# Late modulation vectors as packed rows, reciprocal broadcasts on ScalarE's queue, and a last tile in three pieces

## The chip, the cores and the metric

The kernel runs on one core of a Trainium2 chip. The metric is device time in microseconds of one execution; lower is better. The times shown for a version are medians of repeated runs, and a version's profile comes from one further execution.

## The reference

A transformer block with modulation vectors that depend on a condition c. All large tensors are bfloat16.

```python
mod = silu(c) @ w_mod                     # (1,1024) @ (1024, 6*1024): sa, ca, ga, sb, cb, gb
h = layernorm(x) * (1 + ca) + sa          # x: 2048 x 1024
q = h @ wq                                # 32 heads of 128
p = softmax(q k^T / sqrt(128))            # 4 kv heads, the last 512 keys of the cache
x = x + ga * ((p v) @ wo)                 # wo: 4096 x 1024
h = layernorm(x) * (1 + cb) + sb
x = x + gb * ((silu(h @ w_gate) * (h @ w_up)) @ w_down)   # inner width 3584
```

Six vectors of 1024 values come out of w_mod. sa and ca are needed at once, for the first layernorm. ga is needed when the attention output of the first rows is complete, sb and cb for the second layernorm, and gb only at the very end of the block: these four are the *late* vectors.

## The kernel before

The 2048 rows are worked in four chunks (cc = 0 to 3) of 512 rows, and a chunk in four tiles of 128 rows. Each chunk has 32 attention heads, so the attention part is a loop over 128 steps k, one head of one chunk each (NU = 128, H = 32).

In a step, `emit_s(k)` computes the scores of head k for 512 keys (4 matmuls into two s_ps buffers) and ScalarE turns them into pT by exp. VectorE adds pT up over the keys in two instructions (psA, then psB). `emit_q(k + 3)` computes the queries three heads ahead (8 matmuls of 512 columns, q_ps), and VectorE copies them out of PSUM (qT). `emit_o(k - 1)` multiplies pT by the values (4 matmuls, o_ps), and ScalarE copies o_ps to oT. Every fourth step, `emit_l` sums psB over the partitions for four heads at once: four matmuls with 32 output columns each, every one in its own quarter of the TensorE array and of one PSUM bank (l_ps). ScalarE then takes Ln and Exp of it (the reciprocal, rinv) and stores four rows of it to DRAM (r_d). `load_rb` reads these rows back, repeated over all 128 partitions (rb, two loads of 512 KB), and `emit_norm` on VectorE multiplies oT by rb. From step 12 on, `emit_wo` adds one part of the output projection per step (8 matmuls, a_ps), which VectorE collects in acc.

Other work is hung on the steps through a table of tasks: `at(k, f, ...)` puts a call of f after the queries of step k. In this way are placed: the loads of w_mod (`load_wm`), the late vectors' products (`mod_cols`, `mod_bcast`), the layernorm of the next chunk (`plan_ln`: bn_stats, xn, a DMA transpose into hT, then eight scale-and-shift instructions on VectorE), the loads of x, and an estimate of the scores' bound (`bound_wq`: 32 sums of squares of wq tiles on VectorE, all in chunk 0; `bound_k`: 16 sums of squares of k_ld tiles, at step 10), which decides at the end whether another path of the kernel has to be run.

A column product (`mod_cols`) has 32 matmuls with w_mod as the stationary operand and one moving column. It gives 512 values of a vector as columns (128 partitions x 4), as layernorm's scale and shift are used. A broadcast product (`mod_bcast`) has silu(c), repeated over 128 columns, as the stationary operand (silrep) and w_mod as the moving one; it takes 8 matmuls of 512 columns and gives 512 values on all 128 partitions, as ga and gb are used (ga_bc, gb_bc).

After the attention loop come, chunk by chunk, the gated projections (`emit_gu`: gu_ps, sg, guT) and the down projection (`emit_down`: 28 matmuls into d_ps, then on VectorE f = d_ps * gb and o_sb = f + x, then a store of 128 x 512 values from ScalarE's queue).

The order in which each engine takes its instructions is not that of the code alone. A scheduler places them by priority (the order of the code) and by its own estimate of when they are ready; on the chip each engine then runs its list strictly in order. Tiles come from pools with a fixed number of buffers. The ones that matter here: PSUM tag "mm" with 4 banks, shared by q_ps, o_ps, a_ps, l_ps, d_ps and the modulation products; "hT" with 4 buffers of 1 MB, shared by the w_mod tiles and the hT of the chunks; "rb" with 2; blkB (7 buffers; kT and v_sb hold two of them, and five are left for wq tiles); blkC (10: oT, wo).

Nearly all loads are issued on SyncE's queue, which waits in order for the buffers it fills; in the kernel before, only the load of c and the stores of r_d and of the output are issued by ScalarE.

Of the kernel before, what the change touches and what calls it, by code (L numbers as in the profile page):

```python
# [9 lines left out]
ALU = mybir.AluOpType  # L10
AX = mybir.AxisListType
BF16 = mybir.dt.bfloat16
FP32 = mybir.dt.float32
# [575 lines left out]
def fast_path(ctx, tc, flag, A_x, A_k_cache, A_v_cache, A_wq, A_wo, B_x, B_w_gate, B_w_up,  # L589
# [3 lines left out]
    nc = tc.nc  # L593
    P = 128
    _, S, D = A_x.shape
    _, Hkv, Sk, Dh = A_k_cache.shape
    HD = A_wq.shape[1]
    H = HD // Dh
# [4 lines left out]
    TCW = 512  # L603
    NTC = S // TCW
    QT = TCW // P
    DT = D // P
    FT = F // P
    WT = W // P
    DH = D // 512
# [7 lines left out]
    x2d = A_x.flatten_outer_dims()  # L617
    out2d = out.flatten_outer_dims()
# [5 lines left out]
    wm_v = w_mod.rearrange("(dt p) n -> p dt n", p=P)  # L624
# [4 lines left out]
    const = ctx.enter_context(tc.tile_pool(name="const", bufs=1))  # L629
    xpool = ctx.enter_context(tc.tile_pool(name="xres", bufs=1))  # L630
    hpool = ctx.enter_context(tc.tile_pool(name="hT", bufs=4))
# [3 lines left out]
    wk = ctx.enter_context(tc.tile_pool(name="work", bufs=2))  # L635
    sm = ctx.enter_context(tc.tile_pool(name="small", bufs=4))
    psp = ctx.enter_context(tc.tile_pool(name="psum", bufs=4, space=bass.MemoryType.PSUM))
    dp = ctx.enter_context(tc.tile_pool(name="dram", bufs=4, space=bass.MemoryType.DRAM))
# [7 lines left out]
    def blkC(name, shape, dt=BF16):  # L646
        return pc_.tile(shape, dt, name=name, tag="C")

    def mm(name, shape=(P, 512), dt=FP32):
        return psp.tile(list(shape), dt, name=name, tag="mm", bufs=4)  # L650
# [4 lines left out]
    def load(out, in_, eng=None):  # L655
        with nc.allow_non_contiguous_dma(reason="weight slice"):
            (eng or nc.sync).dma_start(out=out, in_=in_)
# [5 lines left out]
    nc.scalar.dma_start(out=c_r, in_=c_v)  # L663
    xt = [xpool.tile([P, D], BF16, name=f"x{tt}", tag=f"x{tt}") for tt in range(S // P)]

    def load_x(cc):
        for t in range(cc * QT, (cc + 1) * QT):
            nc.sync.dma_start(out=xt[t], in_=x2d[t * P:(t + 1) * P, :])

    wm_tiles = {}  # L670

# [7 lines left out]
    def load_wq(cc, hg, parts=(0, 1)):  # L679
        for i in parts:  # L680
            t = blkB("wq", [P, 4, 512])
            load(t, wq_v[:, 4 * i:4 * i + 4, hg * 512:(hg + 1) * 512])
            wq_tiles[(cc, hg, i)] = t

    load_x(0)
    for half in range(DH):
        load_wm(1, half)
        load_wm(0, half)
# [5 lines left out]
    for kv in range(Hkv):  # L694
        load(v_sb[:, kv], v_v[:, kv])
    load_wq(0, 1)
    load_x(1)


    ident = const.tile([P, P], BF16, name="ident")  # L700
# [1 line left out]
    ones_bf = const.tile([P, P], BF16, name="ones_bf")  # L702
# [4 lines left out]
    sa, ca1, sb, cb1 = (modT[:, i, :] for i in range(4))  # L707
    ga_bc = const.tile([P, D], FP32, name="ga_bc")
    gb_bc = const.tile([P, D], FP32, name="gb_bc")


    ec = sm.tile([DT, P], FP32, name="ec", tag="ec", bufs=2)
    nc.scalar.activation(out=ec, in_=c_r, func=ACT.Exp, scale=-1.0)
    nc.vector.tensor_scalar(out=ec, in0=ec, scalar1=1.0, scalar2=None, op0=ALU.add)
    rc = sm.tile([DT, P], FP32, name="rc", tag="ec", bufs=2)
    nc.vector.reciprocal(out=rc, in_=ec)
    sil_r = const.tile([DT, P], BF16, name="sil_r")
    nc.vector.tensor_tensor(out=sil_r, in0=c_r, in1=rc, op=ALU.mult)
# [2 lines left out]
    siluc = const.tile([P, DT], BF16, name="siluc")  # L721
# [9 lines left out]
        nc.vector.tensor_scalar(out=dst[:, 4 * half:4 * half + 4], in0=ps,  # L731
                                scalar1=1.0 if add_one else 0.0, scalar2=None, op0=ALU.add)

    rep_t = {}

    def mod_bcast(vec, half, dst):
        if "r" not in rep_t:
            r = wk.tile([P, DT, P], BF16, name="silrep", tag="xn", bufs=3)
            for dt in range(DT):
                nc.vector.tensor_scalar(out=r[:, dt, :], in0=ones_bf,  # L740
                                        scalar1=siluc[:, dt:dt + 1], scalar2=None, op0=ALU.mult)
            rep_t["r"] = r
        wm = wm_tiles.pop((vec, half))
        ps = mm("bc_ps")
        for dt in range(DT):
            nc.tensor.matmul(ps, lhsT=rep_t["r"][:, dt, :], rhs=wm[:, dt, :],
                             start=(dt == 0), stop=(dt == DT - 1))
        nc.vector.tensor_copy(out=dst[:, half * 512:(half + 1) * 512], in_=ps)

    tasks = {}  # L750

    def at(k, f, *a):
        tasks.setdefault(k, []).append((f, a))


    hT = {}
# [12 lines left out]
    def ln_norm(tt, on_act=False):  # L769
        mv = ln.pop(tt)  # L770
        n = wk.tile([P, D], BF16, name="xn", tag="xn", bufs=3)
        if on_act:
            nc.vector.scalar_tensor_tensor(out=mv[:, 3:4], in0=mv[:, 0:1], scalar=-1.0,
                                           in1=mv[:, 2:3], op0=ALU.mult, op1=ALU.mult)
            nc.scalar.activation(out=n, in_=xt[tt], func=ACT.Identity, bias=mv[:, 3:4],
                                 scale=mv[:, 2:3])
        else:
            nc.vector.tensor_scalar(out=n, in0=xt[tt], scalar1=mv[:, 0:1], scalar2=mv[:, 2:3],
                                    op0=ALU.subtract, op1=ALU.mult)
        return n  # L780

    xn = {}
# [24 lines left out]
    def plan_ln(k, key, sc, sh):  # L807


        for t in range(QT):  # L810
            tt = key[1] * QT + t
            at(k + 2 * t, ln_stats, tt)
            at(k + 2 * t + 1, ln_rows, tt)
            at(k + 2 * t + 2, ln_xpose, key, tt)
        for dt in range(DT):
            at(k + 11 + dt, ln_mod, key, dt, sc, sh)
# [14 lines left out]
    for t in range(QT):  # L831
        ln_stats(t)
        n = ln_norm(t, t % 2 == 0)
# [4 lines left out]
    for half in range(DH):  # L838
# [6 lines left out]
        for n in range(4 * LEAD):  # L845
            dt, g = (4 * half + n // LEAD, n % LEAD) if half == 0 else (4 + n % 4, n // 4)
            nc.tensor.matmul(q0_ps[g],  # L847
                             lhsT=wq_tiles[(0, 0, dt // 4)][:, dt % 4, g * P:(g + 1) * P],
                             rhs=hT[("h1", 0)][:, dt, :], start=(dt == 0), stop=(dt == DT - 1))
# [111 lines left out]
    def load_rb(g):  # L961
        d = rinv[g // 4]
        rinv[g // 4] = []
        for i in range(2):
            rb = wk.tile([P, 2, TCW], FP32, name="rb", tag="rb", bufs=2)
            nc.sync.dma_start(out=rb, in_=d[2 * i:2 * i + 2, :].partition_broadcast(P))
            rinv[g // 4].append(rb)

    def emit_norm(g):
# [45 lines left out]
            nc.vector.tensor_tensor(out=x1, in0=f, in1=x1, op=ALU.add)  # L1015


    for n, (vec, half) in enumerate(((2, 0), (2, 1), (4, 0), (4, 1), (3, 0), (3, 1), (5, 0), (5, 1))):
        at(1 + 2 * n, load_wm, vec, half)
        if vec in (2, 5):  # L1020
            at(3 + 2 * n, mod_bcast, vec, half, ga_bc if vec == 2 else gb_bc)
        else:
            at(3 + 2 * n, mod_cols, vec, half, cb1 if vec == 4 else sb, vec == 4)
    for cc in range(2, NTC):
        at(4 * (cc - 1) + 12, load_x, cc)
    for hg in range(H // 4):
        for i in range(2):
            for j in range(2):
# [5 lines left out]
        at(g + 2, load_rb, g)  # L1034
        at(g + 4, emit_norm, g)
    for cc in range(1, NTC):
        plan_ln((cc - 1) * H + 2, ("h1", cc), ca1, sa)
    for cc in range(NTC):
        for q in range(NQ):
            s0 = cc * H + q * HQ + HQ + 4  # L1040
# [7 lines left out]
    guT = {}  # L1048
    gu_w = {}
    wd_tiles = {}  # L1050

    def load_gu(cc, fg):
        for nm, v in (("wg", wg_v), ("wu", wu_v)):
            for i in range(2):
                t = blkB(nm, [P, 4, 512])
                load(t, v[:, 4 * i:4 * i + 4, fg * 512:(fg + 1) * 512])
                gu_w[(cc, fg, nm, i)] = t
# [16 lines left out]
    def load_wd(cc, dh, fg):  # L1074
        t = blkC("wd", [P, 4, 512])
        load(t, wd_v[:, 4 * fg:4 * fg + 4, dh * 512:(dh + 1) * 512])
        wd_tiles[(cc, dh, fg)] = t

    def emit_down(cc, dh, t):
        dsl = slice(dh * 512, (dh + 1) * 512)  # L1080
        d_ps = mm("d_ps")
        for f in range(FT):
            nc.tensor.matmul(d_ps, lhsT=guT[(cc, f // 4)][:, f % 4, t * P:(t + 1) * P],  # L1083
                             rhs=wd_tiles[(cc, dh, f // 4)][:, f % 4, :],
                             start=(f == 0), stop=(f == FT - 1))
        r = wk.tile([P, 512], FP32, name="f32", tag="f32", bufs=2)
        nc.vector.tensor_tensor(out=r, in0=d_ps, in1=gb_bc[:, dsl], op=ALU.mult)  # L1087
        o = wk.tile([P, 512], BF16, name="o_sb", tag="row", bufs=5)
        nc.vector.tensor_tensor(out=o, in0=r, in1=xt[cc * QT + t][:, dsl], op=ALU.add)
        row = (cc * QT + t) * P  # L1090
        nc.scalar.dma_start(out=out2d[row:row + P, dsl], in_=o)

    def run_tasks(k):
        for f, a in tasks.pop(k, ()):
            f(*a)
# [15 lines left out]
    for cc in range(NTC):  # L1111
        for fg in range(NFG):
            if (cc, fg) != (0, 0):
                load_gu(cc, fg)
            if cc > 0:
                load_wd(cc, 0, fg)
            for fi in range(4):
                emit_gu(cc, 4 * fg + fi)
                run_tasks(NU + 1 + (cc * NFG + fg) * 4 + fi)
        for dh in range(DH):  # L1120
            if dh > 0 or cc == 0:
                for fg in range(NFG):
                    load_wd(cc, dh, fg)
            for t in range(QT):
                emit_down(cc, dh, t)
    assert not tasks


# [38 lines left out]
```

## Time and profile before

| | |
|---|---|
| median of 10 runs | 1297.7 us (1295.65 to 1299.29) |
| the profiled execution, its own time | 1298.08 us |
| its span in the profile | 1296.3 us |
| TensorE (PE) busy | 1272.6 us, 98% |
| VectorE (DVE) busy | 653.8 us, 50% |
| ScalarE (ACT) busy | 453.9 us, 35% |
| DMA | 220.00 MB, mean 170 GB/s |

The span is what the profiler saw from the first to the last instruction; the profiled execution's own time is 1.8 us longer. PE is TensorE's matmuls, PEld its weight loads (which overlap the matmuls), DVE is VectorE, ACT is ScalarE, SP is SyncE; a q after an engine's name means its queue of DMA issues and waits. A line of a timeline has the start and the length in us, the engine, the kernel's line, the operation with output<-input, the shape, and how many were merged; in square brackets stands the idle time before it and what ended it. Line numbers are those of each version's own kernel.py. A matmul's length in the profile is longer than the time for which it holds TensorE, because matmuls are pipelined: the step from one start to the next is the measure.

### The profile page before, as it was taken

The numbers are of one execution on the slowest core, as the hardware profiler recorded it, in microseconds if no ns is written. First come the engines' busy times: TensorE is split into PE (matmuls) and PEld (weight loads), VectorE is DVE, ScalarE is ACT, GpSimd is POOL, SyncE is SP. The second block draws the span as 40 slices with busy tenths as digits, with TensorE's granted clock in tenths as the row PEclk, the third lists the DMA queues.
The fourth block names the chain that finished last, engine by engine and source line by source line (L and its number), as shares of the span: only waits on it lengthen the run. The fifth ranks groups of instructions, "written<-read, shape, count | busy, mean of one in ns | idle before, by whom it ended". The sixth has DMA issues, their size and how long they took to land.

```text
span 1296.3 us, 15407 instructions
## 1 busy us (share of the span) xinstructions
PE 1272.6 (98%) x6088; PEld 578.1 (45%) x6209; DVE 653.8 (50%) x1143; ACT 453.9 (35%) x646; POOL 0.7 (0%) x6
## 2 busy tenths in 40 slices
PE   6999999999999999999999999999999999999998
PEld 3444444444444444444444444444444444444443
DVE  5999858985569655597554641221222211222122
ACT  3655554555555545555553341001100111011100
POOL 0000000000000000000000000000000000000000
PEclk9999999999999999999999999999999999999999
DMA  9898544564454635355536565454436545453402
GB/s 304 257 353 235 168 147 163 165 181 168 138 169 141 195 128 182 123 163 171 163 131 224 174 219 178 150 191 131 159 110 211 169 142 183 134 191 130 146 24 77
DMA packets 221363, 220.00 MB, mean 170 GB/s; under 512 B 42977, under 2 KB 210913, under 8 KB 221282
## 3 DMA queue, kind: packets, MB, share of 16 engines
q1 hardware_dynamic: 216402, 214.47, 51.9%
q10 hardware_dynamic: 4880, 4.46, 1.0%
q8 instruction: 50, 0.82, 0.3%
q14 instruction: 31, 0.25, 0.1%
HBM read 206.57 MB, written 4.46 MB: 163 GB/s over the span
## 4 chain that ended last, share of the span: by engine, by line
PE 94%; DVE 3%; issue 1%; DMA 1%; ACT 0%; SPq 0%
PE gu_ps L1066 30%; PE a_ps L1000 17%; PE q_ps L922 15%; PE d_ps L1083 15%; PE s_ps L935 8%; PE o_ps L983 7%; PE l_ps L952 1%; DVE junk L862 1%; PE q_ps L847 1%; DMA wm<-in_w_mod_dram 1%; DVE psA L942 1%; DVE st L762 0%; DVE qT L824 0%; PE mod_ps L729 0%; DVE psB L944 0%
## 5 line engine op out<-in xcount | busy, mean ns | idle before, releaser
L937 ACT ACTIVATE pT<-s_ps 128x1024 bf16<-128x1024 f32 x256 | 248.8, 1027 | 8.8 <-PE s_ps L935 5.3
L1000 PE MATMUL a_ps<-wo,oT 128*128 128x512 bf16 x1022 | 242.1, 379 | 0.4
L922 PE MATMUL q_ps<-hT,wq 128*128 128x512 bf16 x996 | 236.7, 379 | 0.4 <-DVE modT L731 0.3
L1071 ACT ACTIVATE sg<-gu_ps 128x512 bf16<-128x512 f32 x112 | 66.9, 597 | 460.3 <-PE gu_ps L1066 451.7
L1072 DVE TENSOR_TENSOR guT<-gu_ps,sg 128x512 bf16<-128x512 f32 x112 | 77.4, 691 | 280.9 <-ACT sg L1071 280.9
L1066 PE MATMUL gu_ps<-hT,wu 128*128 128x512 bf16 x876 | 210.0, 379 | 1.1
L1066 PE MATMUL gu_ps<-hT,wg 128*128 128x512 bf16 x879 | 209.9, 379 | 0.8
L1083 PE MATMUL d_ps<-wd,guT 128*128 128x512 bf16 x879 | 193.1, 379 | 0.9
L985 ACT CAST oT<-o_ps 128x512 bf16<-128x512 f32 x128 | 74.4, 581 | 229.7 <-PE o_ps L983 154.4
L1000 PEld LDWEIGHTS <-oT 128*128 128x128 bf16 x1024 | 100.0, 98 | 121.1 <-DVE oT L973 1.0
L922 PEld LDWEIGHTS <-wq 128*128 128x128 bf16 x1000 | 97.8, 98 | 118.1 <-issue 0.3
L1083 PEld LDWEIGHTS <-guT 128*128 128x128 bf16 x896 | 87.7, 98 | 105.7
L1066 PEld LDWEIGHTS <-wg 128*128 128x128 bf16 x896 | 87.7, 98 | 105.7
L1066 PEld LDWEIGHTS <-wu 128*128 128x128 bf16 x896 | 87.6, 98 | 105.8 <-DMA wu<-in_B_w_up_dram 0.3
L935 PE MATMUL s_ps<-qT,kT 128*128 128x512 bf16 x511 | 131.5, 379 | 2.0 <-ACT pT L937 0.6
L942 DVE TENSOR_TENSOR psA<-pT 128x1024 bf16<-128x1024 bf16 x128 | 87.9, 687 | 75.5 <-ACT pT L937 75.1
L983 PE MATMUL o_ps<-pT,v_sb 128*128 128x512 bf16 x454 | 123.9, 380 | 1.7 <-issue 0.2
L824 DVE CAST qT<-q_ps 128x512 bf16<-128x512 f32 x128 | 87.6, 686 | 53.8 <-PE q_ps L922 51.4
L1087 DVE TENSOR_TENSOR f<-d_ps,gb_bc 128x512 f32<-128x512 f32 x32 | 22.1, 692 | 148.4 <-PE d_ps L1083 148.4
L973 DVE TENSOR_TENSOR oT<-oT,rb 128x1024 bf16<-128x1024 bf16 x64 | 77.9, 1222 | 22.0 <-DMA rb<-r_d 21.8
L935 PEld LDWEIGHTS <-kT 128*128 128x128 bf16 x512 | 50.1, 98 | 61.4 <-issue 1.3
L983 PEld LDWEIGHTS <-v_sb 128*128 128x128 bf16 x512 | 47.2, 98 | 59.5 <-issue 7.3
(70 smaller groups left out, 495.0 us busy)
## 6 DMA issues: line engine op xcount, KB each, us to landing
wq<-in_A_wq_dram SPq DMA_DIRECT2D x64, 512.0 KB
rb<-r_d SPq DMA_DIRECT2D x64, 512.0 KB
wo<-in_A_wo_dram SPq DMA_DIRECT2D x64, 512.0 KB
wg<-in_B_w_gate_dram SPq DMA_DIRECT2D x56, 512.0 KB
wu<-in_B_w_up_dram SPq DMA_DIRECT2D x56, 512.0 KB
wd<-in_B_w_down_dram SPq DMA_DIRECT2D x56, 512.0 KB
wm<-in_w_mod_dram SPq DMA_DIRECT2D x12, 1024.0 KB
x<-in_A_x_dram SPq DMA_DIRECT2D x16, 256.0 KB
```

Of the source, the lines that this page charges most:

```text
L824: nc.vector.tensor_copy(out=t, in_=q_ps)
L922: nc.tensor.matmul(q_ps, lhsT=wq_tiles[(cc, h // 4, dt // 4)][:, dt % 4, (h % 4) * P:(h % 4 + 1) * P], rhs=hT[("h1", cc)][:, dt, :], start ...
L935: nc.tensor.matmul(s_ps[:, i, :], lhsT=kT[:, kv, j * P:(j + 1) * P], rhs=qT[g], start=True, stop=True)
L937: nc.scalar.activation(out=p[:, 2 * jj:2 * jj + 2, :], in_=s_ps, func=ACT.Exp, scale=scale)
L942: nc.vector.tensor_tensor(out=a, in0=p[:, 0:2, :], in1=p[:, 2:4, :], op=ALU.add)
L973: nc.vector.tensor_tensor(out=oo, in0=oo, in1=rb, op=ALU.mult)
L983: nc.tensor.matmul(o_ps, lhsT=v_sb[:, kv, j, :], rhs=pT[g][:, j, :], start=(j == 0), stop=(j == WT - 1))
L985: nc.scalar.copy(out=oT[(cc, hg)][:, hi, :], in_=o_ps)
L1000: nc.tensor.matmul(a_ps, lhsT=oT[(cc, 2 * q + i)][:, hh % 4, t * P:(t + 1) * P], rhs=wo_tiles[(cc, q, dh, i)][:, hh % 4, :], start=(hh == ...
L1066: nc.tensor.matmul(ps[:, n, :], lhsT=gu_w[(cc, fg, nm, dt // 4)][:, dt % 4, fi * P:(fi + 1) * P], rhs=hT[("h2", cc)][:, dt, :], start=(dt ...
L1072: nc.vector.tensor_tensor(out=guT[(cc, fg)][:, fi, :], in0=ps[:, 1, :], in1=g, op=ALU.mult)
L1083: nc.tensor.matmul(d_ps, lhsT=guT[(cc, f // 4)][:, f % 4, t * P:(t + 1) * P], rhs=wd_tiles[(cc, dh, f // 4)][:, f % 4, :], start=(f == 0), ...
```

## The change

1. The late vectors are no longer computed by four column products and four broadcasts of 8 and 32 matmuls. `load_rows` loads 4 of the 8 row blocks of two vectors (two tiles of 1 MB), and `mod_rows` multiplies them by silu(c) repeated over 32 columns (sil32): 4 rounds of four matmuls, each of the four in its own 32-column quarter, so that one PSUM bank gets four rows of 512 values. Two passes make two vectors: the first is copied to SBUF (row), the second is added to it. The four rows are stored to DRAM (row_d); `load_gate` reads a vector back over all partitions, `load_cols` reads one back as columns. The passes are hung on steps 5 and 13 (ga, cb) and 21 and 29 (gb, sb).
2. sil32 is filled at the start by eight VectorE instructions; silrep goes.
3. The loads of x are hung on single steps instead of groups of four. Chunk 1's are no longer issued before the loop but on steps 2, 4, 6 and 8.
4. The layernorm of chunk 1 starts at step 10 instead of 2.
5. The last 128 x 512 output tile is computed in pieces of 256, 128 and 128 columns.
6. ec and rc are taken from another buffer.
7. The loads of rb are issued from ScalarE's queue instead of SyncE's.

```diff
-    def load_x(cc):
-        for t in range(cc * QT, (cc + 1) * QT):
-            nc.sync.dma_start(out=xt[t], in_=x2d[t * P:(t + 1) * P, :])
+    def load_x(tt):
+        nc.sync.dma_start(out=xt[tt], in_=x2d[tt * P:(tt + 1) * P, :])
...
     load_wq(0, 1)
-    load_x(1)
...
-    ec = sm.tile([DT, P], FP32, name="ec", tag="ec", bufs=2)
+    ec = wk.tile([DT, P], FP32, name="ec", tag="f32", bufs=2)
...
-    def mod_bcast(vec, half, dst):
...
+    sil32 = const.tile([P, DT, 32], BF16, name="sil32")
+    for dt in range(DT):
+        nc.vector.tensor_scalar(out=sil32[:, dt, :], in0=ones_bf[:, 0:32],
+                                scalar1=siluc[:, dt:dt + 1], scalar2=None, op0=ALU.mult)
...
+    def load_rows(vecs, part):
+        wm_rows.append([])
+        for vec in vecs:
+            t = hpool.tile([P, 4, D], BF16, name="wmr", tag="hT")
+            load(t, wm_v[:, 4 * part:4 * part + 4, vec * D:(vec + 1) * D])
+            wm_rows[-1].append(t)
+
+    def mod_rows(n, part):
+        ps = mm("row_ps")
+        tiles = wm_rows.pop()
+        for k in range(4):
+            for i in range(4):
+                nc.tensor.matmul(ps[32 * i:32 * i + 32, :], lhsT=sil32[:, 4 * part + k, :],
+                                 rhs=tiles[i // 2][:, k, (i % 2) * 512:(i % 2 + 1) * 512],
+                                 start=(k == 0), stop=(k == 3))
+        if part == 0:
+            r = blkC("row", [P, TCW], FP32)
+            nc.vector.tensor_copy(out=r, in_=ps)
+            row_part.append(r)
+        else:
+            r = row_part.pop()
+            nc.vector.tensor_tensor(out=r, in0=ps, in1=r, op=ALU.add)
+            d = dp.tile([4, TCW], FP32, name="row_d", tag="row_d", bufs=2)
+            nc.sync.dma_start(out=d, in_=r[0:P:32, :])
+            row_d[n] = d
+
+    def load_gate(n, k, dst):
+        nc.sync.dma_start(out=dst.rearrange("p (a b) -> p a b", a=2),
+                          in_=row_d[n][k:k + 2, :].partition_broadcast(P))
+
+    def load_cols(n, k, dst, add_one):
+        src = row_d[n][k:k + 2, :].rearrange("a (b p) -> p (a b)", p=P)
...
+            nc.sync.dma_start(out=dst, in_=src)
+        if add_one:
+            nc.vector.tensor_scalar(out=dst, in0=dst, scalar1=1.0, scalar2=None, op0=ALU.add)
...
             rb = wk.tile([P, 2, TCW], FP32, name="rb", tag="rb", bufs=2)
-            nc.sync.dma_start(out=rb, in_=d[2 * i:2 * i + 2, :].partition_broadcast(P))
+            nc.scalar.dma_start(out=rb, in_=d[2 * i:2 * i + 2, :].partition_broadcast(P))
...
-    for n, (vec, half) in enumerate(((2, 0), (2, 1), (4, 0), (4, 1), (3, 0), (3, 1), (5, 0), (5, 1))):
-        at(1 + 2 * n, load_wm, vec, half)
-        if vec in (2, 5):
-            at(3 + 2 * n, mod_bcast, vec, half, ga_bc if vec == 2 else gb_bc)
-        else:
-            at(3 + 2 * n, mod_cols, vec, half, cb1 if vec == 4 else sb, vec == 4)
-    for cc in range(2, NTC):
-        at(4 * (cc - 1) + 12, load_x, cc)
+    for n, vecs in enumerate(((2, 4), (5, 3))):
+        for part in range(2):
+            k = 16 * n + 8 * part + 1
+            at(k, load_rows, vecs, part)
+            at(k + 4, mod_rows, n, part)
+        at(16 * n + 15, load_gate, n, 0, gb_bc if n else ga_bc)
+        at(16 * n + 16, load_cols, n, 2, sb if n else cb1, n == 0)
+    for tt in range(QT, S // P):
+        cc, t = divmod(tt, QT)
+        at(max((cc - 1) * H - 16, 0) + 2 + 2 * t, load_x, tt)
...
-        plan_ln((cc - 1) * H + 2, ("h1", cc), ca1, sa)
+        plan_ln((cc - 1) * H + (10 if cc == 1 else 2), ("h1", cc), ca1, sa)
...
-    def emit_down(cc, dh, t):
+    def emit_down(cc, dh, t, widths=(512,)):
...
+        for w in widths:
+            dsl = slice(dh * 512 + c0, dh * 512 + c0 + w)
+            d_ps = mm("d_ps", (P, w))
...
-                emit_down(cc, dh, t)
+                last = cc == NTC - 1 and dh == DH - 1 and t == QT - 1
+                emit_down(cc, dh, t, (256, 128, 128) if last else (512,))
```

More of the change, by code (lines that the diff above doesn't have):

```diff
@@ L683, in load_wq @@
             wq_tiles[(cc, hg, i)] = t
-    load_x(0)
+    for tt in range(QT):
+        load_x(tt)
     for half in range(DH):
@@ L709, in fast_path @@
     gb_bc = const.tile([P, D], FP32, name="gb_bc")
-    ec = sm.tile([DT, P], FP32, name="ec", tag="ec", bufs=2)
+    ec = wk.tile([DT, P], FP32, name="ec", tag="f32", bufs=2)
     nc.scalar.activation(out=ec, in_=c_r, func=ACT.Exp, scale=-1.0)
     nc.vector.tensor_scalar(out=ec, in0=ec, scalar1=1.0, scalar2=None, op0=ALU.add)
-    rc = sm.tile([DT, P], FP32, name="rc", tag="ec", bufs=2)
+    rc = wk.tile([DT, P], FP32, name="rc", tag="f32", bufs=2)
     nc.vector.reciprocal(out=rc, in_=ec)
@@ L732, in mod_cols @@
                                 scalar1=1.0 if add_one else 0.0, scalar2=None, op0=ALU.add)
-    rep_t = {}
-    def mod_bcast(vec, half, dst):
[L737 to L748, printed above, removed]
+    sil32 = const.tile([P, DT, 32], BF16, name="sil32")
@@ new lines, in fast_path @@
+    for dt in range(DT):
+        nc.vector.tensor_scalar(out=sil32[:, dt, :], in0=ones_bf[:, 0:32],
+                                scalar1=siluc[:, dt:dt + 1], scalar2=None, op0=ALU.mult)
+    wm_rows = []
+    row_part = []
+    row_d = {}
+    def load_rows(vecs, part):
[4 more added lines that the diff above has]
+            wm_rows[-1].append(t)
@@ new lines, in load_gate @@
+    def load_gate(n, k, dst):
[3 more added lines that the diff above has]
+        src = row_d[n][k:k + 2, :].rearrange("a (b p) -> p (a b)", p=P)
+        with nc.allow_non_contiguous_dma(reason="1024 values to columns"):
+            nc.sync.dma_start(out=dst, in_=src)
+        if add_one:
+            nc.vector.tensor_scalar(out=dst, in0=dst, scalar1=1.0, scalar2=None, op0=ALU.add)
@@ L1077, in load_wd @@
         wd_tiles[(cc, dh, fg)] = t
-    def emit_down(cc, dh, t):
[L1080 to L1089, printed above, removed]
-        row = (cc * QT + t) * P
-        nc.scalar.dma_start(out=out2d[row:row + P, dsl], in_=o)
+    def emit_down(cc, dh, t, widths=(512,)):
+        row = (cc * QT + t) * P
+        c0 = 0
+        for w in widths:
+            dsl = slice(dh * 512 + c0, dh * 512 + c0 + w)
+            d_ps = mm("d_ps", (P, w))
+            for f in range(FT):
+                nc.tensor.matmul(d_ps, lhsT=guT[(cc, f // 4)][:, f % 4, t * P:(t + 1) * P],
+                                 rhs=wd_tiles[(cc, dh, f // 4)][:, f % 4, c0:c0 + w],
+                                 start=(f == 0), stop=(f == FT - 1))
+            r = wk.tile([P, w], FP32, name="f32", tag="f32", bufs=2)
+            nc.vector.tensor_tensor(out=r, in0=d_ps, in1=gb_bc[:, dsl], op=ALU.mult)
+            o = wk.tile([P, w], BF16, name="o_sb", tag="row", bufs=5)
+            nc.vector.tensor_tensor(out=o, in0=r, in1=xt[cc * QT + t][:, dsl], op=ALU.add)
+            nc.scalar.dma_start(out=out2d[row:row + P, dsl], in_=o)
+            c0 += w
     def run_tasks(k):
```

## The prediction

> **What bounds the kernel now.** I read the page's busy times first, then the timeline by engine, the stretches of 10 us, and the wait lists.
>
> ```profile
> PE 1272.6 (98%) x6088; PEld 578.1 (45%) x6209; DVE 653.8 (50%) x1143; ACT 453.9 (35%) x646; POOL 0.7 (0%) x6
> L748 DVE COPY ga_bc<-bc_ps 128x512 f32<-128x512 f32 x2 | 1.4, 688 | 0.0
> ...
> 70.00:80.00 10.00, 9.95 (x77) 4.74 (x76) 10.00 (x48) 6.35 (x9) 0.00 (x0) 1.00 1.10 365
> ...
> 150.00:160.00 10.00, 9.95 (x47) 4.51 (x46) 7.33 (x13) 4.93 (x7) 0.00 (x0) 1.00 0.65 203
> ```
>
> TensorE is busy throughout, and the last group's 0.0 idle says that VectorE never waited for those copies. The columns of a stretch are PE, PEld, DVE, ACT, POOL, clock, DMA share and GB/s: at 70 us VectorE is at 10.00 of 10 too, at 150 us no longer. A busy TensorE can hide idle slots, so I took the starts:
>
> ```profile
> 39.77 1.89 PE L746 MATMUL bc_ps<-wm,silrep 128*128 128x512 bf16 x8
> 41.50 1.03 PE L983 MATMUL o_ps<-pT,v_sb 128*128 128x512 bf16 x4
> 45.05 0.40 PE L952 MATMUL l_ps<-psB,ones_bf 128*32 128x512 bf16 x4
> 45.38 1.04 PE L983 MATMUL o_ps<-pT,v_sb 128*128 128x512 bf16 x4
> ...
> 57.48 0.94 PE L729 MATMUL mod_ps<-siluc,wm 128*128 128x1 bf16 x32
> 58.28 1.02 PE L983 MATMUL o_ps<-pT,v_sb 128*128 128x512 bf16 x4
> ...
> 78.54 0.48 PE L952 MATMUL l_ps<-psB,ones_bf 128*32 128x512 bf16 x4
> ```
>
> From one start to the next, 8 full matmuls take 1.73 us (216 ns each), a column pass (32 mod_ps) 0.80, and an l_ps group 0.42 (its q_ps ended at 44.96). From 31 to 1290 us the starts leave under 1 us of idle TensorE: in this kernel every TensorE microsecond removed is a gain, unless something else is late. What is nearest to late stands in VectorE's timeline:
>
> ```profile
> 76.88 0.70 DVE L942 TENSOR_TENSOR psA<-pT 128x1024 bf16<-128x1024 bf16 x1
> ...
> 77.56 0.69 DVE L824 CAST qT<-q_ps 128x512 bf16<-128x512 f32 x1
> 78.16 0.43 DVE L944 TENSOR_TENSOR psB<-psA 128x512 bf16<-128x512 bf16 x1
> ...
> 89.70 0.69 DVE L942 TENSOR_TENSOR psA<-pT 128x1024 bf16<-128x1024 bf16 x1 [0.23 <-ACT pT L937]
> ```
>
> VectorE has no idle time from 30.70 until the 0.23 us at 89.7. The psB at 78.16 is what the stretched l_ps group at 78.54 (0.48 us, not 0.40) waited for: **there TensorE had just caught up with VectorE.**
>
> **The Trainium skill.** "TensorE: Matmul & The Clock Gate", Part 3, lets four matmuls of 32 output columns run together, about 4 ns apart: the trace agrees (four in 0.40 us). "TensorEngine Tiling (Array Packing)", Key Properties, says a change of tiling mode drains the array: it agrees too, 0.42 us against 0.22 for one matmul. The first page, Part 1, gives N/2.4 GHz plus 2.5 ns per warm matmul: 216 ns at 512 agrees; its 56 ns at 128 is in no warm stretch here. "DMA: Bandwidth & Descriptors", Anatomy of one DMA, says that a DMA's wait is served on the issuing sequencer; SyncE's 123.7 us of waits for r_d ahead of rb agree. In the changed kernel ScalarE stands there.
>
> **Part by part.**
>
> *Removed from TensorE:* four broadcasts, 4 x 1.73 = 6.9 us, and the four late column products, 4 x 0.80 = 3.2. Sum 10.1, all on the path.
>
> *Added:* four row passes of 4 quartets. By the l_ps group, 4 x 0.216 + 0.21 for the two drains = 1.07 us each, 4.3 in all. No run shows new weights loaded into a column tile while it streams: exposed they cost about 0.1 us a quartet (the PEld row of l_ps has 92 ns), 6.0 in all; fully serial, 16 x 0.216 each, 14.6. Below 4 x 0.86 = 3.5 it can't go. I take 4.3.
>
> *VectorE, the cover that goes.* The built order of the changed kernel puts in front of the psB of step 11, against before: 3 xn less (start to start 0.46 each), 1 bn_stats less (0.59), 2 aggregates less (0.12 each), one copy less (0.60), 2 modT less (0.07 each), and 2 oT normalisations more (1.13 each): only 0.7 us earlier. TensorE gets there with 2 broadcasts and 3 column products less (5.9), one pass more (1.1), and 2.1 us of other matmuls taken ahead (4 of a_ps, an l_ps part, 4 of s_ps): 2.7 us earlier. o_ps of step 11 waits for the PSUM bank of the q_ps whose qT copy stands behind the 16 k_ld sums (0.21 each) and psA: it stalls 2.7 - 0.7 = 2.0 us, and the next q_ps 0.5 more for ScalarE's Ln of that l_ps. Net of the 0.3 us that before loses just after (an a_ps waiting for oT), I charge 2.3. From there I ran VectorE's list on by the same intervals against TensorE's: two more bank waits, for an acc and a qT copy at steps 16 to 20, cost 0.7. Sum **+3.0**; at least 0 (if the waits fall elsewhere), at most the 5.8 net saving. h1's later start is thus no gain of its own; its deadline, step 29, is 50 us after its last hT operation in the order.
>
> *rb on ScalarE's queue.* Each group of 4 heads adds two issues, 0.37 us each (SyncE's median), behind two exps. r_d to rb took 1.7 us in the steady stretch, and ScalarE reaches rb 0.48 + 2.05 = 2.5 us after r_d: no wait. While DMA is full (steps 8 to 24) it was 3.6 to 5.0, so ScalarE stands up to 2.5 us, with the next exps and o_ps copies queued behind. A step is 5.3 us and its exps take 2.05, so TensorE sees nothing; with that cover gone, the three or four groups concerned would cost up to 2.5 us each. VectorE's oT, in order, then waits for rb: rb takes some 4 us to land (5.8 - 1.7, steady), so it is there 6.5 to 8 us after r_d; VectorE arrives 6.4 to 9 after. I take +0.7 (0 to 6). SyncE, freed of these waits, only issues wq and wo sooner, which their buffers limit.
>
> *Other moves on queues.* On SyncE come two 8 KB row_d stores, two gate broadcasts of 512 KB and two column loads of 1024 single values, each behind a wait for the row copy; wq and wo queued behind them have 15 us and more before use. The x loads spread out, and as much of w_mod is loaded as before. I take 0; the lead of the weight loads is the cover, and where it is gone TensorE waits for one landing, 2 to 5 us by the r_d and rb intervals. The row tile takes one of the ten blkC buffers in steps 5 to 13 and 21 to 29, where by the code at most nine others are held: 0. The new buffers of ec and rc, and the free xn buffer, touch nothing on the path: 0.
>
> *Start.* Eight sil32 fills (0.07 to 0.17 us each by the modT and silrep intervals) now stand before the first xn instead of in VectorE's idle 12.4 us point, and 8 h_ps transposes (0.86 us) behind the second mod_ps. I take +0.4 (-0.3 to +1.2; the start runs partly at half clock).
>
> *End.* The last f and o_sb take 0.69 each at 512 columns; at 128 about 0.30 (straight line from modT's 0.16 at 4): -0.8. TensorE: 28 x (110 + 56 + 56) ns against 28 x 216: +0.15. By the cold h_ps row (0.11 us for 128 columns) it would be +3. 128-column stores have 256-byte rows: 0 to +0.6. Taken -0.65 (-1.0 to +2.2).
>
> **Sum:** -10.1 + 4.3 + 3.0 + 0.7 + 0.4 - 0.65 = -2.35 us. The profiled execution took 1298.08 (span 1296.3 and 1.8 around it), 0.4 over the median of the ten runs; it would go to 1295.7, and the median of 1297.7 to **1295.4**. About 0.2%, 2.6 us, is what a measurement here can tell from no change.
>
> **Rivals.**
>
> *VectorE doesn't bind* (0.24): the bank waits fall into slack. -10.1 + 4.3 + 0.4 - 0.65, some 1291.7. For it: outside 30 to 130 us VectorE idles. Against it: the 0.48 us group at 78.54.
>
> *rb comes late (the slower side)* (0.22): ScalarE's issue, one exp pair later than SyncE's, finds full DMA queues at the groups of steps 5 to 17, and VectorE, without slack there, passes each wait on to TensorE. Arrival 6.7, 8.1, 6.4 and 9.0 us after r_d; if rb takes 9, the waits are 2.3 + 0.9 + 2.6 + 0 = 5.8 instead of 0.7: 1300.5. It decides from 8 us on. For it: up to 5.0 us from r_d to rb before. Against it: rb no longer stands behind 512 KB loads on one queue.
>
> *The column tiles don't overlap with new weights* (0.06): serial passes cost 10.3 more, 1305.7. Against it: the l_ps group.
>
> *Not what it says:* the built order has four passes of 16 and no broadcast; this is excluded.
>
> **The numbers.** My case has 0.48, with 1293 to 1297.8 as its own range: 0.19 faster, 0.26 same, 0.03 slower. VectorE free: 0.22 faster, 0.02 same. rb late: 0.06 same, 0.16 slower. Serial: 0.06 slower. Faster 0.41, same 0.34, slower 0.25. 1290.6 to 1300.8 leaves out the serial passes, and the far ends of the start and the tail.
>
> **What would show it.** Right: row_ps groups of about 0.9 us busy, each 1.07 from start to start; a gap of some 2 us before an o_ps matmul near 76 us, released by a qT copy; VectorE at 10 of 10 to about 125 us; no ScalarE wait that TensorE shares after 150 us. Wrong: oT waits on rb over 3 us in sum before 130 us (rb late); no gap near 76 us (VectorE free); row_ps groups over 2 us (serial); last output later than 5.9 us after the last matmul (end).

## The result, and the profile after

The changed kernel takes **1323.9 us** (median of 8 runs, 1321.8 to 1327.9), the kernel before 1297.8 (28 runs): ratio **1.0209, 95% interval 1.0199 to 1.0219**. It is slower by 26 us, where 1295.4 was forecast and 1300.8 was the upper end of the range. Its profiled execution took 1320.36 us, 3.5 less than the median, with a span of 1318.6 us against 1296.3; what follows is read from that one execution.

First the page of the kernel before, then that of the changed kernel: the chain of waits by engine and the group of normalisations, whose last column is VectorE's idle time before them and what ended it; for the changed kernel the busy times too.

```profile
PE 94%; DVE 3%; issue 1%; DMA 1%; ACT 0%; SPq 0%
...
L973 DVE TENSOR_TENSOR oT<-oT,rb 128x1024 bf16<-128x1024 bf16 x64 | 77.9, 1222 | 22.0 <-DMA rb<-r_d 21.8
```

```profile
PE 1279.2 (97%) x6050; PEld 577.7 (44%) x6169; DVE 651.6 (49%) x1144; ACT 454.6 (34%) x646; POOL 0.7 (0%) x6
...
PE 85%; DMA 7%; DVE 5%; issue 2%; ACT 1%; ACTq 0%; SPq 0%; DVEq 0%
...
L1004 DVE TENSOR_TENSOR oT<-oT,rb 128x1024 bf16<-128x1024 bf16 x64 | 78.2, 1221 | 73.1 <-DMA rb<-r_d 73.0
```

The chain had 94% TensorE and 1% DMA before; now 7% is DMA. The normalisations waited 21.8 us for rb before, now 73.0. Total busy times hardly moved, so they don't show the loss. The stretches do (columns as in the prediction), before and after:

```profile
60.00:80.00 20.00, 19.73 (x151) 9.56 (x153) 20.00 (x68) 13.98 (x20) 0.00 (x0) 1.00 1.08 343
80.00:100.00 20.00, 19.75 (x119) 9.13 (x120) 19.74 (x35) 8.26 (x12) 0.00 (x0) 1.00 0.96 349
...
180.00:200.00 20.00, 19.89 (x95) 8.90 (x95) 14.15 (x32) 10.93 (x14) 0.00 (x0) 1.00 0.49 164
```

```profile
60.00:80.00 20.00, 17.78 (x74) 7.31 (x74) 14.65 (x28) 11.07 (x16) 0.00 (x0) 0.91 0.78 169
80.00:100.00 20.00, 14.84 (x62) 4.69 (x61) 17.79 (x57) 4.84 (x9) 0.00 (x0) 0.74 0.70 231
...
180.00:200.00 20.00, 16.98 (x87) 7.01 (x87) 9.79 (x20) 7.60 (x11) 0.00 (x0) 0.95 1.00 236
```

Before, TensorE was busy 19.7 to 20.0 of 20 us in every stretch from 40 to 200 us. It is now idle 15.1 us more over these 160 us, and the granted clock (0.91, 0.74, 0.95, and 0.97 in 200 to 220) takes up to another 0.09 + 0.26 + 0.05 + 0.03 = 0.43 of 20 us, 8.6 us, less what of it falls on idle time. The starts of o_ps, one per step, say what this comes to: steps 0 to 32 take 183.0 us against 163.4 before, though some 6 us of TensorE's work were removed there. From 220 to 690 us TensorE runs as before; 2.4 us more are lost at the end of the attention loop, where TensorE is busy 18.58 of 20 us in 700 to 720. VectorE, at 20.00 of 20 from 40 to 80 us before, is at 14.6: it is not the bound, it stands.

What it stands for is in the timeline of the first group (start, duration, engine, operation; in brackets the idle time ahead and its releaser):

```profile
44.38 4.66 SPq L657 DMA_DIRECT2D wmr<-in_w_mod_dram  x2
...
45.49 0.58 ACTq L989 DMA_DIRECT2D r_d<-rinv  x1
...
49.09 4.08 SPq L657 DMA_DIRECT2D k_ld<-in_A_k_cache_dram  x4
...
50.50 1.34 ACTq L997 DMA_DIRECT2D rb<-r_d  x2
...
51.23 1.23 DVE L893 SCALAR_TENSOR_TENSOR junk<-wq 128x1024 bf16<-128x1024 bf16 x1
51.88 0.59 ACT L1016 CAST oT<-o_ps 128x512 bf16<-128x512 f32 x1 [3.82 <-issue]
...
57.89 1.23 DVE L1004 TENSOR_TENSOR oT<-oT,rb 128x1024 bf16<-128x1024 bf16 x1 [5.42 <-DMA rb<-r_d]
59.04 0.68 DVE L855 CAST qT<-q_ps 128x512 bf16<-128x512 f32 x1
...
59.77 0.59 PE L953 MATMUL q_ps<-hT,wq 128*128 128x512 bf16 x2 [1.58 <-DVE qT L855]
```

ScalarE's copy stood 3.82 us: ScalarE waited for r_d until 50.50 and then issued the two rb, 1.34 us. Meanwhile SyncE, which no longer waits for r_d, issued a second wmr (1 MB) and k_ld. VectorE came to the normalisation at 52.5 and waited 5.42 us; the qT copy behind it was late, and TensorE waited 1.58 us for that. More such gaps follow, and then this:

```profile
64.52 0.38 PE L983 MATMUL l_ps<-psB,ones_bf 128*32 128x512 bf16 x1 [1.16 <-DVE psB L975]
64.83 1.89 PE L1014 MATMUL o_ps<-pT,v_sb 128*128 128x512 bf16 x4
66.51 1.86 PE L966 MATMUL s_ps<-qT,kT 128*128 128x512 bf16 x4
68.21 1.89 PE L953 MATMUL q_ps<-hT,wq 128*128 128x512 bf16 x8
```

Four matmuls take 1.68 us from start to start where four took 0.86: half clock for 3.4 us, after gaps of 1.58, 1.00 and 1.16 us. At 68.21 eight are back to 1.73. "TensorE: Matmul & The Clock Gate", Part 1, of the Trainium skill halves the clock after an idle window of about 3.4 us, and tells of a kernel whose frequent short pauses made its clock swing too. Here no gap is that long; what counts is how much of a stretch of 3.41 us is idle:

| stretch of the changed kernel, us | TensorE busy | clock after it |
|---|---|---|
| 57.95 to 61.37 (the gap of 1.58) | 1.84 us | full |
| 61.37 to 64.78 (1.00 and 1.16) | 1.24 us | half |
| 81.85 to 85.26 | 1.52 us | half |

In each of the fourteen traces the granted clock changes only at multiples of 3.41 us from each other. With the time from 30 to 1280 us divided there, all fourteen changes from full to half clock follow a stretch in which TensorE was idle for 1.86 us or more, and none of the other stretches at full clock has more than 1.77. So a wait costs more than itself: here about one and a half times, 15.1 us of idle time and up to 8.6 us of clock.

### The profile page after: what moved, and what is told of

Same layout as the page of the kernel before. It is cut to its first block, busy times and chain, and to the rows that moved or that the text cites. A ratio compares the mean times of both kernels' runs of the same rounds, so it can differ in the third digit from the quotient of the medians.

```text
span 1318.6 us, 15323 instructions
## 1 busy us (share of the span) xinstructions
PE 1279.2 (97%) x6050; PEld 577.7 (44%) x6169; DVE 651.6 (49%) x1144; ACT 454.6 (34%) x646; POOL 0.7 (0%) x6
## 4 chain that ended last, share of the span: by engine, by line
PE 85%; DMA 7%; DVE 5%; issue 2%; ACT 1%; ACTq 0%; SPq 0%; DVEq 0%
PE gu_ps L1099 29%; PE d_ps L1119 15%; PE a_ps L1031 14%; PE q_ps L953 13%; PE o_ps L1014 7%; PE s_ps L966 6%; DMA rb<-r_d 2%; DMA r_d<-rinv 1%; DMA hT<-xn 1%; DVE psA L973 1%; PE q_ps L878 1%; PE l_ps L983 1%; DVE st L793 1%; DVE oT L1004 1%; DMA row_d<-row 1%
## 5 line engine op out<-in xcount | busy, mean ns | idle before, releaser
L1119 PE MATMUL d_ps<-wd,guT 128*128 128x512 bf16 (+2 forms) x935 | 193.3, 366 | 0.9
L1014 PE MATMUL o_ps<-pT,v_sb 128*128 128x512 bf16 x507 | 133.5, 385 | 5.8 <-DVE acc L1039 3.0
L1119 PEld LDWEIGHTS <-guT 128*128 128x128 bf16 x952 | 90.9, 98 | 103.0
L966 PE MATMUL s_ps<-qT,kT 128*128 128x512 bf16 x512 | 134.8, 385 | 1.1 <-ACT pT L968 1.0
L1123 DVE TENSOR_TENSOR f<-d_ps,gb_bc 128x512 f32<-128x512 f32 (+2 forms) x34 | 22.5, 660 | 147.0 <-PE d_ps L1119 147.0
```

Of the source, the lines that this page charges most:

```text
L966: nc.tensor.matmul(s_ps[:, i, :], lhsT=kT[:, kv, j * P:(j + 1) * P], rhs=qT[g], start=True, stop=True)
L1014: nc.tensor.matmul(o_ps, lhsT=v_sb[:, kv, j, :], rhs=pT[g][:, j, :], start=(j == 0), stop=(j == WT - 1))
```

## The experiments

Theory A: rb on a queue of its own lands late. Rival B: the row scheme, its 2 MB loads and the later LayerNorm stall VectorE. All ratios are to the kernel before on the same chip, with 95% intervals.

**One part at a time.** e1_rb_sync is the changed kernel with

```
-            nc.scalar.dma_start(out=rb, in_=...)
+            nc.sync.dma_start(out=rb, in_=...)
```

> The changed kernel with one part undone: rb is issued by SyncE again. Theory A (rb on ScalarE's own queue runs beside SyncE's loads on the same 16 DMA engines and lands late): the wait of oT on rb falls from 73 us in total to about 20, TensorE's windows 40:160 and 180:200 go back to about 19.8 of 20 us, and the time comes to 1295 to 1299 us, some 25 us below the changed kernel. Theory B (the row scheme, with its 2 MB loads every eight steps, and the later LayerNorm are what stalls VectorE): rb is still late in the first 60 steps, and the time stays within 6 us of the changed kernel's 1324. A time between 1303 and 1316 would say that both are needed.

Measured 1296.6 us, 0.9988 (0.9978 to 0.9998): all of the loss is gone, the wait on rb is 20.5 us. Rival B falls as the explanation of the 26 us. e2_rb_act_only is the kernel before with the opposite edit.

> The kernel before with rb issued by ScalarE and nothing else changed. Theory A: slower than before, by 15 to 28 us if the queue alone does it, with oT's wait on rb at 50 us or more. Theory B: within 5 us of before (the prediction's own price was +0.7, 0 to 6). If A is right about the mechanism but needs the changed kernel's loads beside it, some 3 to 10 us slower.

1315.5 us, 1.0137 (1.0108 to 1.0167), wait on rb 75.0 us: the queue alone does 17 us, without rows, and the other parts raise that to 27. e3_ln_early is the changed kernel with `plan_ln((cc - 1) * H + 2, ...)` for every chunk.

> The changed kernel with the LayerNorm of chunk 1 at steps 2 to 20 again in place of 10 to 28. Theory A: nothing to speak of, within 6 us of 1324 (VectorE's LayerNorm work only lies elsewhere). Theory B, if the LayerNorm's place is what collides: the gaps of 80 to 160 us shrink and it is 10 us or more faster than the changed kernel.

1315.1 us, 1.0139 (1.0120 to 1.0158): 9 us better, between what the theories expected. The later LayerNorm adds to the damage, but doesn't cause it. How is not shown: in this run VectorE's list also has the first two groups' normalisations two psB later than in the changed kernel, and steps 4 to 8 take 14.8 us against 21.4. e6_sync_ln_early has both edits.

> rb on SyncE again and the LayerNorm of chunk 1 at steps 2 to 20 again; the rest of the changed kernel stays. The run with rb on SyncE alone came to 1296.6 with some 3.5 us of TensorE lost in 60:80, 120:140 and 180:200. If these come from the later LayerNorm, 1293 to 1295 here; if from the row passes' loads, 1296 to 1298 again; if early LayerNorm and the k_ld sums collide as in the kernel before, 1297 to 1300.

1298.8 us, 1.0010 (1.0001 to 1.0020): with rb on SyncE the early place is 2 us worse, as in the third expectation. e4_tail_only is the kernel before with the widths (256, 128, 128) for the last tile.

> The kernel before with only the last output tile in pieces of 256, 128 and 128 columns. The prediction's term is -0.65 us (-1.0 to +2.2): about 1297, so no difference that can be told from before. In the trace the time from the last matmul to the end of the span should be some 0.9 us shorter and the last tile's matmuls some 0.25 us longer. No theory of the loss puts any of it here; 1.5 us or more slower would mean that part of the loss sits at the end.

1297.2 us, 0.9996 (0.9988 to 1.0005). From last matmul to end of span 5.29 us against 5.93; the last tile's matmuls 0.14 longer (1283.49 to 1289.64, against 1284.36 to 1290.37). Net -0.5.

**Why does the queue matter?** The same stretch with rb on SyncE:

```profile
50.89 0.81 SPq L997 DMA_DIRECT2D rb<-r_d  x2
...
51.74 2.08 SPq L657 DMA_DIRECT2D k_ld<-in_A_k_cache_dram  x4
...
52.91 0.70 DVE L855 CAST qT<-q_ps 128x512 bf16<-128x512 f32 x1
...
53.51 0.43 DVE L975 TENSOR_TENSOR psB<-psA 128x512 bf16<-128x512 bf16 x1
...
55.12 1.23 DVE L1004 TENSOR_TENSOR oT<-oT,rb 128x1024 bf16<-128x1024 bf16 x1
```

Two things differ. *The hold*: k_ld and the second wmr now stand behind rb, because SyncE's wait for r_d holds them. The first packet of rb's first half starts 1.0 us after its issue and the last one ends 3.4 after; on ScalarE's queue these were 3.4 and 5.9. *The place*: the two normalisations of the first group stand after the seventh and the eighth psB in VectorE's list, on ScalarE's queue both after the sixth; those of the second group after the twelfth in place of the tenth. Copies that TensorE needs now stand ahead of them. The list is built for an estimated landing; that for a free queue it reckoned with an earlier one is inferred from the places, no run shows the estimate.

Both matter, for the wait is the difference of two times: when rb's first half has landed (its semaphore is complete), and when VectorE comes to it. In us after the issue of r_d, for the first three groups (e5_norm_held and e7_rb_pool come below):

| | rb landed | VectorE came | VectorE waited |
|---|---|---|---|
| the prediction | 6.5 to 8 | 6.7, 8.1, 6.4 | 0.7 in all |
| before | 9.3, 9.0, 9.1 | 11.2, 16.1, 12.6 | 0, 0, 0 |
| changed | 12.4, 13.1, 8.4 | 7.0, 7.3, 7.0 | 5.4, 5.8, 1.4 |
| e1_rb_sync | 10.3, 9.4, 8.9 | 10.3, 15.8, 9.3 | 0, 0, 0 |
| e5_norm_held | 12.4, 11.8, 6.1 | 14.8, 18.3, 13.3 | 0, 0, 0 |
| e7_rb_pool | 12.2, 13.1, 12.2 | 7.1, 15.2, 7.2 | 5.2, 0, 5.0 |

In the kernel before rb did not land early either, but VectorE came later still:

```profile
56.63 0.42 DVE L944 TENSOR_TENSOR psB<-psA 128x512 bf16<-128x512 bf16 x1
...
58.23 1.18 DVE L973 TENSOR_TENSOR oT<-oT,rb 128x1024 bf16<-128x1024 bf16 x1
```

With the landings of before and VectorE's times of the changed kernel, the three waits would be 2.3 + 1.7 + 2.1 = 6.1 us, an estimate from the table, where they were 12.6: place and landing have about equal shares in them.

e5_norm_held leaves rb on ScalarE and moves the place of the first eight groups:

```
+            hold = 4 if g < 8 else 3 if g < 32 else 0
+            if hold:
+                nc.vector.scalar_tensor_tensor(out=rb[:, 0, 0:1], in0=rec[g + hold][:, 0:1], scalar=0.0,
+                                               in1=rb[:, 0, 0:1], op0=ALU.mult, op1=ALU.add)
```

> The changed kernel, rb still on ScalarE, but with the normalisations of the first eight groups held behind the fourth or third psB after their group (a one-column VectorE operation that reads that psB and rewrites one column of rb with its own value), so that they stand in VectorE's list where the kernel before has them or a place later. Theory A1 (the loss comes from the place in the list: with rb on its own queue the list was laid out for an earlier landing, and VectorE, in order, stands before rb with copies behind it that TensorE needs): the wait on rb before 200 us falls under 5 us in all and the time to 1296 to 1302. Theory A2 (rb lands so late on ScalarE's queue that no place within reach helps): 1310 or more, with TensorE then waiting for oT itself at a_ps. About 1305 to 1310 would share it.

1309.7 us, 1.0104 (1.0084 to 1.0123): the shared case. VectorE no longer waits for rb before 215 us. Half of the loss, 14.2 us, is back. e7_rb_pool issues rb by `nc.gpsimd.dma_start`.

> The changed kernel with rb issued by GpSimd, which has nothing else to do here. It is again a queue of its own beside SyncE's, so SyncE's loads are not held back, but VectorE's list has the second halves of the first groups one or two places later than with rb on ScalarE (nearly the list of the run with rb on SyncE). Theory A1 (place in the list): 1297 to 1305. Theory A2 (any queue beside SyncE's makes rb late): 1312 to 1326. If GpSimd's own issue takes long (not shown in any run so far), rb lands later still and it is 1326 or more.

1321.7 us, 1.0182 (1.0165 to 1.0199). Its list is nearly that of e1_rb_sync (the first group's normalisations stand one psB earlier). In the second group, where VectorE comes late, it doesn't wait; in the first and the third it does, for rb lands late. So the loss isn't ScalarE's own: another queue beside SyncE's has it too. Nor does the queue alone make rb late: in e5_norm_held, on ScalarE's queue, the third group's lands 6.1 us after r_d. Late loads and a standing VectorE go together; no run separates which makes which.

e8_act_gate puts back the hold, with rb on ScalarE:

```
+        gate = sm.tile([1, 4], FP32, name="gate", tag="gate", bufs=2)
+        nc.sync.dma_start(out=gate, in_=d[0:1, 0:4])
```

> The changed kernel, rb on ScalarE, with VectorE's list as in the changed kernel; but SyncE issues a 16-byte read of r_d for each group, at the place in the program where it issued rb before, so that its loads are again held until r_d has landed. Theory A2a (SyncE's loads, no longer held behind the wait for r_d, get in front of rb on the DMA engines): rb's first packet starts about 1 us after its issue in the first groups instead of about 3, and the time falls to 1300 to 1312, the rest being the early place in the list. Theory A2b (what matters is only that the two queues share the engines, not who is held): within 5 us of 1324.

1315.0 us, 1.0121 (1.0093 to 1.0149): 9 us better. The first packet of the first group starts 1.0 us after issue, as expected; the time is 3 us above the upper end. e9_act_gate_held has the hold and the place.

> Both: SyncE's loads held by the 16-byte read, and the normalisations of the first eight groups held to a later place in VectorE's list; rb still on ScalarE. If place and unheld loads are the whole of it: 1296 to 1301, as with rb on SyncE. If the two queues sharing the engines costs something by itself: 1303 to 1310, as with the place alone (1309.7).

1307.8 us, 1.0083 (1.0066 to 1.0100). The second expectation, so something was missing. The starts of o_ps show where: from step 0 to step 28 this kernel takes 141.2 us, with rb on SyncE 139.3; from 28 to 32 it takes **31.2 against 22.7**. Its timeline there:

```profile
162.48 5.82 SPq L822 DMA_TRANSPOSE hT<-xn  x3
...
169.13 1.23 ACTq L999 DMA_DIRECT2D rb<-r_d  x2
169.60 1.23 SPq L822 DMA_TRANSPOSE hT<-xn  x1
...
182.24 0.73 DVE L829 TENSOR_SCALAR hT<-hT,modT 128x512 bf16<-128x512 bf16 x2 [11.42 <-DMA hT<-xn]
...
183.62 1.86 PE L1021 MATMUL o_ps<-pT,v_sb 128*128 128x512 bf16 x4 [7.57 <-DVE acc L1046]
```

The four DMA transposes of h1 of chunk 2 go out together, and the 1 MB of rb of the group g = 27 goes out beside them. VectorE waits 11.42 us for the last transpose, and an acc copy behind it holds TensorE for 7.57. e11_gate_held_27 changes one group:

```
+            eng = nc.sync if g == 27 else nc.scalar
+            eng.dma_start(out=rb, in_=...)
```

> As the run with both holds (rb on ScalarE, SyncE's loads held by the 16-byte read, the first eight groups' normalisations held), but the two rb loads of the one group g = 27 are issued by SyncE. That run kept step with the run that has rb on SyncE up to step 28 and then took 31.2 us for steps 28 to 32 against 22.7. Theory A3 (there the four DMA transposes of h1 of chunk 2, released together by the last row pass, share the DMA engines with rb of g = 27, which on SyncE's own queue stands behind them): steps 28 to 32 take 22 to 24 us and the time is 1296 to 1301. If the transposes are slow for another reason, it stays at 1304 to 1309.

1300.0 us, 1.0019 (1.0012 to 1.0025); steps 28 to 32 take 21.4 us:

```profile
172.59 1.23 SPq L822 DMA_TRANSPOSE hT<-xn  x1
...
174.36 0.35 SPq L1000 DMA_DIRECT2D rb<-r_d  x1
...
177.64 0.73 DVE L829 TENSOR_SCALAR hT<-hT,modT 128x512 bf16<-128x512 bf16 x2 [3.86 <-DMA hT<-xn]
```

From the last transpose's issue to VectorE's next operation 5.0 us, against 12.6. One detail of the expectation was wrong: the last row pass doesn't release the transposes. In the changed kernel three of them are issued 181 to 187 us, the pass starts at 186.71, and the first of them had waited for a q_ps, the last reader of chunk 0's hT.

**So the 27.3 us of rb's queue** go, in the order of these runs: 16.0 with place and hold together (1323.9 to 1307.8), 7.8 with the group g = 27 moved (to 1300.0), and 3.4 that no run splits further (to 1296.6). These are differences of medians from different chips, good to some 2 us. Of the last 3.4, TensorE's waits for ScalarE's exps show 1.8 (2.4 us against 0.6 with rb on SyncE).

That is how they came back, and not how the changed kernel lost them. The starts of o_ps in one profiled execution of each tell that (us; those of the changed kernel and of e5_norm_held were 3.5 and 4.3 faster than their medians):

| | steps 0 to 28 | 28 to 32 | 32 to 127 |
|---|---|---|---|
| before | 142.3 | 21.2 | 494.8 |
| changed | 157.0 | 26.0 | 497.6 |
| e1_rb_sync | 139.3 | 22.7 | 494.8 |
| e5_norm_held (place) | 141.4 | 24.6 | 498.6 |
| e8_act_gate (hold) | 145.4 | 33.0 | 495.5 |
| e9_act_gate_held (both) | 141.2 | 31.2 | 495.8 |
| e11_gate_held_27 | 141.6 | 21.4 | 495.5 |

Against e1_rb_sync the changed kernel loses 17.7 us in the first 28 steps, 3.3 in the next four and 2.8 after them. Of the 17.7 the place alone brings back 15.6, the hold alone 11.7, both 15.8: once VectorE doesn't stand, the hold adds next to nothing. And it seems to have a price: with it steps 28 to 32 take 33.0 and 31.2 us, without it 26.0 and 24.6. Most of the 7.8 that e11_gate_held_27 saves came in with the hold, then; why the hold makes the meeting with the transposes dearer is open.

**A version a little faster than both.** e10_sync_k_act is e1_rb_sync with the sums of k_ld on ScalarE:

```
-            nc.vector.scalar_tensor_tensor(out=junk, in0=src, scalar=1.0, in1=src, op0=ALU.mult,
-                                           op1=ALU.mult, accum_out=kk[:, i:i + 1])
+            nc.scalar.activation(out=junk, in_=src, func=ACT.Square, accum_out=kk[:, i:i + 1])
```

> rb on SyncE again, and the 16 sums of squares of k_ld move from VectorE to ScalarE (Square with a sum), which was busy 13 of 20 us there. The prediction's third step says that VectorE, filled by these sums, makes TensorE wait some 3 us near 76 us, of which 1.9 us were seen at 60:80 in the run with rb on SyncE alone. If so, that gap goes and the time is 1293.5 to 1296; if the gap comes from elsewhere, or ScalarE's exponentials get late instead, 1296 to 1299.

1296.1 us, 0.9986 (0.9979 to 0.9993); TensorE is busy 18.02 of 20 us in 60:80, no more than the 18.35 with the sums on VectorE:

```profile
73.18 1.02 PE L1013 MATMUL o_ps<-pT,v_sb 128*128 128x512 bf16 x4 [0.85 <-DVE qT L855]
75.33 0.38 PE L982 MATMUL l_ps<-psB,ones_bf 128*32 128x512 bf16 x1 [0.91 <-DVE psB L974]
```

The wait is still there with the sums gone from VectorE, so it doesn't rest on them alone; what takes their place, ScalarE (16.6 of 20 us) among others, is not separated. e12_rows_every6 has `k = 6 * (2 * n + part) + 1` as well.

> The best so far (rb on SyncE, sums of k_ld on ScalarE, 1296.1) with the row passes every six steps in place of every eight, so that the last one frees its two buffers six steps earlier and the transposes of h1 of chunk 2 are not all issued at one place. If the 1.5 us that TensorE lost at 160:180 come from that bunch: 1294 to 1296, otherwise 1295.5 to 1298; the 2 MB loads then lie closer to the full DMA engines of 60 to 100 us, which could take it back.

1296.0 us, **0.9980 (0.9971 to 0.9988)**, the best. The loss at 160:180 is gone (20.00), and 1.3 and 0.9 us are lost at 100:120 and 120:140 instead. It can't be told from 1296.1.

## Why the prediction was wrong, point by point

- **Removed and added TensorE work: right.** A row pass takes 0.98 us from start to start (1.07 predicted):

```profile
47.59 1.05 PE L756 MATMUL row_ps<-wmr,sil 128*32 128x512 bf16 x16
48.57 1.04 PE L1014 MATMUL o_ps<-pT,v_sb 128*128 128x512 bf16 x4
```

  With rb on SyncE, steps 0 to 4 take 16.2 us against 18.6: two broadcasts less, one pass more, 2 x 1.73 - 0.98 = 2.5. The serial rival is out.
- **VectorE becomes the bound, +3.0: size near, mechanism partly.** Without the rb term the forecast was -3.05 us; e1_rb_sync gave -1.5. TensorE's waits in 20 to 260 us are 5.2 us there and 1.4 before, 3.8 more. (In the working, 2.0 + 0.5 - 0.3 is 2.2, not 2.3.) Near 76 us it waits 1.03 for a psB and 0.51 for an oT, not 2.0 for a qT copy; moving the k_ld sums away didn't close the gap.
- **rb on ScalarE's queue, +0.7 (0 to 6): the step that failed.** It measured 27.3 with the rest of the change, 17 alone. VectorE's times were forecast well (6.7, 8.1 and 6.4 us after r_d, measured 7.0, 7.3 and 7.0). The landing was not: "6.5 to 8 us after r_d" was 12.4 and 13.1 in the first two groups, and 9.3 and 9.0 already in the kernel before. "Rb takes some 4 us to land" was read where the DMA engines are half idle; from its issue the first half took 7.4 and 11.3 us here, and r_d itself 4.5 in the first group. And "SyncE, freed of these waits, only issues wq and wo sooner, which their buffers limit" was wrong: it issued wmr and k_ld ahead of rb, which the wait for r_d had been holding back. "DMA: Bandwidth & Descriptors" of the Trainium skill, Issuing engines are not separate DMA queues, says that transfers of SyncE and ScalarE run on the same 16 engines and interleave; the runs fit (1.0 us to rb's first packet with SyncE's loads held back, 3.4 without), and the prediction used only the issuing side. What a wait costs was mis-sized too: the 12.9 us of waits before 130 us cost TensorE more than themselves, through the half clock, and the meeting with the transposes was not foreseen.
- **"TensorE sees nothing" of ScalarE's stand**: nearly right, 1.8 us more waiting for exps in e11_gate_held_27 than with rb on SyncE.
- **The rival "rb comes late"** named the wait and its sign: the waits on rb before 130 us came to 12.9 us, against 5.8 in the rival and 0.4 before. Its price was low, 1300.5, for it let rb land 9 us after r_d, passed each wait on once, and knew neither of the half clock nor of the transposes at step 28.
- **Other queue moves, 0: right** within what e1_rb_sync can tell. **End, -0.65: near** (-0.5 in the trace of e4_tail_only, where matmuls of 256 and 128 columns start 109 and 56 ns apart, about as the sum had them). **Start, +0.4:** not told; the first o_ps of kernels with the same start lies between 29 and 32 us.

## What to carry to other kernels

Where a list is built for an engine that works in order, moving a load to another queue can also move its consumer forward, and the engine then stands in front of it with everything behind; compare the place of the consumer in the two lists, and price the wait, not the instruction. Ask too what the load's wait was holding back on the old queue: those transfers now start first and share the DMA engines with it. Putting such a hold back can cost elsewhere, as it did here at step 28. Read a landing time in the stretch where the DMA engines are full, not in the steady one.

## What the runs showed of the hardware

- TensorE's clock was halved for one or more stretches of 3.41 us after a stretch in which it was idle 1.86 us or more, in several short gaps as well as in one; with 1.77 us or less it stayed full (all fourteen traces, 30 to 1280 us). It came back after a half-clock stretch with 0.62 us or less idle, and stayed at half with 1.01 or more.
- Four DMA transposes were issued beside 1 MB of plain loads from another queue in six kernels: from the last one's issue to VectorE's use of it 8.1 to 14.8 us passed (8.3 in the changed kernel, 12.6 in e9_act_gate_held). In the four kernels where those loads stood behind it on the same queue it was 4.8 to 5.2.
- The last packet of the same 512 KB load came 4.2 us after its issue on SyncE's queue, 5.3 on ScalarE's and 6.1 on GpSimd's (mean of the first halves of the first seven groups, changed kernel with only the queue differing). It is not a property of the queue alone: on ScalarE's queue it was 4.2 when the normalisations stood later (e5_norm_held).
- Sixteen matmuls of 512 columns in four 32-column quarters, with new weights for each, took 0.98 us from start to start, less than the 1.07 of the estimate: loading new weights cost nothing that the trace shows.
